# Top-k attention and squared-ReLU feed-forward: pair maxima from PSUM and SBUF, quad maxima by a reduction

## The chip, the core and the metric

The kernel runs on one core of a Trainium2 chip. The metric is the device time of one execution in microseconds; the time stated for the kernel is the median of three runs. The profile is that of one execution, taken by the hardware profiler.

## The reference

`q`, `k` and `v` have the shape 8 x 8 x 576 x 64 (batches, heads, positions, head size), in float32.

```python
scores = (1 / sqrt(64)) * q @ k.transpose(0, 1, 3, 2)      # 576 x 576 for each head
kth    = np.partition(scores, -32, axis=-1)[..., -32:-31]   # 32nd largest of each row
scores = np.where(scores >= kth, scores, -1e9)
attn   = softmax(scores)                                    # over the 32 that are left
x      = (attn @ v), heads side by side                     # 4608 x 512
out    = relu(x @ w_in) ** 2 @ w_out                        # 512 -> 2048 -> 512
```

## The kernel before

The kernel is not written as a program for each engine. It makes a list of operations (`pl.op`: engine, planned duration, priority, the tiles that it reads, writes and takes), and `Plan.schedule` runs through a plan of time in which each engine takes the ready operation with the lowest priority number whose tiles are free. The order that comes out is fixed: each engine's queue is then emitted in that order, with the semaphore waits that the tiles call for. So a planned duration changes no instruction, but it can change the order of every queue, and at run time each engine works through its queue strictly in turn.

**Blocks and groups.** A block is 128 rows of one head's score matrix (the last 64 rows of two heads share a block), so it is a tile of 128 x 576. Two heads make a pair, with nine blocks: three groups of two blocks and one group of three. There are 32 pairs, thus 128 groups and 288 blocks.

**The scores.** For each group TensorE computes the scores into PSUM, two banks for each block (288 columns in each; tiles `ss`), with priority `tg - 30`, and ScalarE copies each block to SBUF (tile `s`, L458). PSUM has eight banks, and all other matmuls (transposes, masked scores, `attn @ v`, both feed-forward products) use the same eight. There are eight `s` buffers; one is held until the mask `w` is made from it (L561).

**The 32nd largest (`top_k`, L426).** The 576 scores of a row are halves A and B.
- VectorE takes `m = max(A, B)` (L522, 288 columns), and GpSimd adds the bit patterns of A and B as integers (`t1`), so that `t1 - m` is later the smaller one of each pair.
- VectorE takes `pp`, the maximum of the two halves of `m` (L528, 144 columns), and GpSimd adds the two halves of `m` as integers (`t2`).
- The tile `f` holds 144 quad maxima, 144 losers of the second comparison (`t2 - pp`) and 288 losers of the first (`t1 - m`), the last two written by GpSimd.
- VectorE finds the eight largest of 144 (L539) and replaces them (L541), again over 144, then over 288, then the last eight over all 576 (L547, L550, L553). The last gives `kth`. One comparison at the end of the program tells whether the shortcut held for all rows; a slower second plan stands behind a branch.

The GpSimd operations are all emitted by the helper at L514. There are four buffers of `m`, `pp` and `f`, and two of `t1` and `t2`.

**The rest.** ScalarE makes `w = relu(kth - s)` (L561). `attend` computes the scores once more, transposed, adds the steep penalty of `w` by a matmul, and exponentiates (L620, L633); `attn @ v` follows, its normalisation on VectorE and GpSimd (L661, L663), and a transpose. `feed` runs the feed-forward for a batch (L698 to L741). VectorE's operations in `top_k` have rising priorities from `tg`, so a group's are planned after those of the group before.

Of the kernel before, what the change touches and what calls it, by code (L numbers as in the profile page):

```python
# [5 lines left out]
ALU = mybir.AluOpType  # L6
ACTF = mybir.ActivationFunctionType
AX = mybir.AxisListType
# [12 lines left out]
class Pool:  # L21
# [16 lines left out]
    def find(self, width):  # L38
        if width == 1:
            if not self.free:  # L40
                return None
            if self.name == "psum":
                half = [s for s in self.free if (s ^ 1) not in self.free]
                s = half[0] if half else self.free[0]
            else:
                s = self.free[0]
            self.free.remove(s)
            return s
        for s in self.free:
            if s % width == 0 and all(s + i in self.free for i in range(width)):  # L50
                for i in range(width):
                    self.free.remove(s + i)
                return s
        return None
# [21 lines left out]

class Op:
    __slots__ = ("eng", "dur", "prio", "fn", "deps", "tiles", "takes", "n", "users", "start", "end",
                 "idx", "sem", "val", "ndma", "seq", "vc", "waits", "wars", "later", "nbf")


ENGS = ("pe", "act", "dve", "gp", "sp")
# [2 lines left out]
class Plan:  # L85
    def __init__(self):
        self.ops = []

    def op(self, eng, dur, prio, fn, r=(), w=(), u=(), hold=(), take=(), after=(), order=(), sem=None, ndma=0, nbf=0.0):


        o = Op()
        o.eng, o.dur, o.prio, o.fn = eng, dur, prio, fn
        o.sem, o.ndma, o.seq, o.nbf = sem, ndma, len(self.ops), nbf
        o.takes = list(take)
        o.users = []
        o.start = o.end = o.idx = o.val = o.vc = None
        deps = set(after)
        for t in r:
            deps.update(t.writers)  # L100
        for t in u:
            deps.update(t.ops)
        for t in list(r) + list(w) + list(u) + list(hold):
            t.ops.append(o)
            t.left += 1
        for t in list(w) + list(u):
            t.writers.append(o)
        for t in o.takes:
            t.taker = o
        o.later = ({t.taker for t in list(r) + list(w) + list(u) + list(hold)} | set(order)) - deps - {o, None}  # L110
        o.deps = deps
        o.wars = list(w) + list(u)
        o.tiles = list(r) + list(w) + list(u) + list(hold)
        self.ops.append(o)
        return o

    def schedule(self, t0=0.0, latency=0.12, own=0.07):
# [7 lines left out]
        busy = {e: t0 for e in ENGS}  # L125
        order = {e: [] for e in ENGS}
# [11 lines left out]
        push(t0, "go", None)  # L138
        readyat = {o: t0 + o.nbf for o in self.ops}
        done = 0  # L140
        while events:
            t = events[0][0]
            while events and events[0][0] <= t + 1e-9:
                _, _, kind, x = heapq.heappop(events)
                if kind == "end":
                    done += 1
                    for tl in x.tiles:
                        tl.left -= 1
                        if tl.left == 0 and tl.slot is not None:
                            for i in range(tl.width):  # L150
                                tl.pool.last[tl.slot + i] = tl
                            tl.pool.give(tl.slot, tl.width)
                    for v in x.users:
                        left[v] -= 1
                        lat = own if v.eng == x.eng else latency
                        readyat[v] = max(readyat[v], t + lat)
                        if left[v] == 0:
                            push(readyat[v], "ready", v)
                elif kind == "ready":
                    heapq.heappush(ready[x.eng], (x.prio, x.seq, x))  # L160
            for e in ENGS:
                if busy[e] > t + 1e-9:
                    continue
                skipped = []
                while ready[e]:
                    item = heapq.heappop(ready[e])
                    o = item[2]
                    got = []
                    ok = True
                    for tl in o.takes:  # L170
                        s = tl.pool.take(tl)
                        if s is None:
                            ok = False
                            break
                        got.append((tl, s))
                    if not ok:
                        for tl, s in got:
                            tl.pool.undo(s, tl.width)
                        skipped.append(item)
                        continue  # L180
                    for tl, s in got:
                        tl.slot = s
                        tl.prev = []
                        for i in range(tl.width):
                            p = tl.pool.last[s + i]
                            if p is not None:
                                tl.prev.append(p)
                    o.start = t
                    hold = o.dur if e != "sp" else 0.6 * o.ndma
                    o.end = t + o.dur + (hold if e == "sp" else 0)  # L190
                    busy[e] = t + hold
                    order[e].append(o)
                    push(busy[e], "go", None)
                    push(o.end, "end", o)
                    break
                for item in skipped:
                    heapq.heappush(ready[e], item)
# [79 lines left out]
def bass_top_k_attn__then__act_relu_squared_kernel(  # L277
# [8 lines left out]
    NB, H, S, D = q.shape  # L286
    assert H == 8 and S == 576 and D == 64, (NB, H, S, D)
    HALF, QUART = S // 2, S // 4
# [49 lines left out]
    def at(t):  # L338
        return mem[t.pool.name][t.slot]

    def bank(t, i=0):
        return ps32[:, t.slot + i, :]
# [11 lines left out]
                {3: ([2, 3], True), 0: ([0], False), 1: ([1], False)}, [(256, 320), (0, 128), (128, 128)])  # L354

    PER = 3.2
    T0 = 12.0

    def mm(o, l, r, start, stop=True):
# [5 lines left out]
    def build(full, weights, pl):  # L365
# [60 lines left out]
        def top_k(gi, qk, tg, dw):  # L426
# [27 lines left out]
            pl.op("pe", 1.2, tg - 30, scores, r=[qk], w=ss[:2], take=ss[:2] + st[:2])  # L454
            if nb == 3:
                pl.op("pe", 1.2, tg - 29, scores_last, r=[qk], w=[ss[2]], take=[ss[2], st[2]])
            for i in range(nb):
                pl.op("act", .64, tg - 28 + i, lambda i=i: act.copy(  # L458
                    at(st[i])[:, :].rearrange("p (a c) -> p a c", a=2),
                    ps32[:, ss[i].slot:ss[i].slot + 2, 0:HALF]), r=[ss[i]], w=[st[i]])  # L460

            a = tile("a")
            dk = [0]
# [1 line left out]
            state["g"] += 1  # L465
            state["z"] += nb == 3

            def dve(dur, fn, **kw):
                dk[0] += 1
                return pl.op("dve", dur, tg + .34 * dk[0], fn, **kw)  # L470

            def eighth(t, i):

# [35 lines left out]
            else:  # L509
# [3 lines left out]
                def whole(dur, prio, i, op, o, x, y, **kw):  # L513
                    return pl.op("gp", dur, prio + .8 * i, lambda: gp.tensor_tensor(  # L514
                        o().bitcast(I32), x().bitcast(I32), y().bitcast(I32), op), **kw)

                low, mid = [], []
                for i in range(nb):
                    A, B = (lambda i=i: at(st[i])[:, 0:HALF]), (lambda i=i: at(st[i])[:, HALF:S])
                    M, L = (lambda i=i: at(m[i])[:, :]), (lambda i=i: at(t1[i])[:, :])  # L520
                    whole(.81, tg - 1, i, ALU.add, L, A, B, r=[st[i]], w=[t1[i]], take=[t1[i]])
                    dve(.42, lambda i=i, A=A, B=B: vec.tensor_tensor(at(m[i])[:, :], A(), B(), ALU.max),  # L522
                        r=[st[i]], w=[m[i]], take=[m[i]])
                for i in range(nb):
                    M1, M2 = (lambda i=i: at(m[i])[:, 0:QUART]), (lambda i=i: at(m[i])[:, QUART:HALF])
                    Q, L = (lambda i=i: at(pp[i])[:, :]), (lambda i=i: at(t2[i])[:, :])
                    whole(.46, tg - .5, i, ALU.add, L, M1, M2, r=[m[i]], w=[t2[i]], take=[t2[i]])
                    dve(.27, lambda i=i, M1=M1, M2=M2: vec.tensor_tensor(at(pp[i])[:, :], M1(), M2(), ALU.max),  # L528
                        r=[m[i]], w=[pp[i]], take=[pp[i], f[i]] + ([a] if i == 0 else []))
                for i in range(nb):  # L530
                    mid.append(whole(.48, tg + .5, i, ALU.subtract, lambda i=i: at(f[i])[:, QUART:HALF],
                                     lambda i=i: at(t2[i])[:, :], lambda i=i: at(pp[i])[:, :],
                                     r=[t2[i], pp[i]], w=[f[i]]))
                    low.append(whole(.88, tg + 2.5, i, ALU.subtract, lambda i=i: at(f[i])[:, HALF:S],
                                     lambda i=i: at(t1[i])[:, :], lambda i=i: at(m[i])[:, :],
                                     r=[t1[i], m[i]], w=[f[i]]))
                prev = [[] for _ in range(nb)]
# [379 lines left out]
```

## Time and profile before

| what | us |
|---|---|
| median of three runs | 1082.91 (1082.89 to 1084.41) |
| the profiled execution | 1080.87 |
| its span, first to last instruction | 1079.0 |
| VectorE busy | 980.8 |
| TensorE busy | 918.1 |
| GpSimd busy | 906.7 |
| ScalarE busy | 765.9 |

Busy is the time in which at least one instruction of the engine is in the record; successive instructions of VectorE and GpSimd overlap a little in the records, so that the distance from one start to the next is shorter than the duration of one. Durations below are those of the records unless it is said that they are distances.

### The profile page before, as it was taken

To read this page: it belongs to the slowest core of one execution; us is meant where nothing else is said; L and a number is where in the kernel's file an instruction comes from. 1 tells how busy PE (TensorE), PEld (TensorE's weight loads), DVE (VectorE), ACT (ScalarE), POOL (GpSimd) and SP (SyncE) were. 2 spreads that over 40 slices of the span, in tenths; PEclk is the share of its full clock that TensorE was granted. 3 is DMA by queue.
4 is the path that set the end of the run, shared out by engine and by line. 5 is a ranking of instruction groups with operands and counts; after the bars stand their busy time and mean duration, and the time that the engine had idled before them with its cause. 6 is when DMAs were issued, how large, how long until landed. Compare 5 with 4: busy or idle time off the path is not lost.

```text
span 1079.0 us, 23727 instructions
## 1 busy us (share of the span) xinstructions
PE 918.1 (85%) x8035; PEld 548.5 (51%) x8082; DVE 980.8 (91%) x3538; ACT 765.9 (71%) x1341; POOL 906.7 (84%) x1391
## 2 busy tenths in 40 slices
PE   6766868788899998889888899898888998979897
PEld 4434435444555555545455445555455554644554
DVE  5999999599999999599999999799998899999951
ACT  5645658766698678867688777887688776656652
POOL 7998989689988898588897999789897799999871
PEclk9878789999999999999899999999999999898999
DMA  6533310220200112112110013001220100000001
GB/s 146 130 101 100 111 46 13 56 54 21 71 12 12 53 48 57 23 42 54 28 45 2 24 51 93 23 2 52 67 50 1 44 21 16 2 1 21 21 16 38
DMA packets 124419, 47.77 MB, mean 44 GB/s; under 512 B 116608, under 2 KB 116608, under 8 KB 124288
## 3 DMA queue, kind: packets, MB, share of 16 engines
q1 hardware_dynamic: 124288, 46.16, 16.6%
q8 instruction: 65, 1.06, 0.4%
q14 instruction: 66, 0.54, 0.2%
HBM read 36.70 MB, written 9.44 MB: 43 GB/s over the span
## 4 chain that ended last, share of the span: by engine, by line
DVE 59%; POOL 13%; PE 12%; issue 10%; ACT 5%; SPq 0%; DMA 0%; POOLq 0%; DVEq 0%
DVE kth L553 15%; PE ps L360 12%; DVE c L547 11%; DVE m L522 10%; DVE f L550 8%; POOL f L514 7%; DVE pp L528 7%; POOL t L514 5%; DVE f L541 4%; DVE a L539 3%; ACT w L561 2%; ACT s L458 1%; POOL x L663 1%; PE ps L363 1%; DVE rzall L661 1%
## 5 line engine op out<-in xcount | busy, mean ns | idle before, releaser
L360 PE MATMUL ps<-qk 64*128 64x288 f32 (+7 forms) x2640 | 434.4, 443 | 60.7 <-ACT w L561 19.3
L561 ACT ACTIVATE w<-s,kth 128x576 bf16<-128x576 f32 x288 | 214.5, 771 | 137.3 <-DVE kth L553 136.9
L360 PEld LDWEIGHTS ps<-qk 64*128 64x128 f32 (+1 forms) x2640 | 216.4, 185 | 178.6 <-ACT w L561 33.3
L514 POOL TENSOR_TENSOR t<-s 128x288 int32<-128x288 int32 x288 | 234.0, 823 | 33.0 <-ACT s L458 30.5
L514 POOL TENSOR_TENSOR f<-t,m 128x288 int32<-128x288 int32 x288 | 228.1, 807 | 0.0
L514 POOL TENSOR_TENSOR t<-m 128x144 int32<-128x144 int32 x288 | 180.8, 638 | 49.9 <-DVE m L522 47.8
L550 DVE MATCH_REPLACE8 f<-c,f 128x144 f32<-128x144 f32 (+1 forms) x576 | 206.4, 363 | 0.0
L553 DVE MAX8 kth<-f 128x8 f32<-128x576 f32 x288 | 202.9, 742 | 2.6 <-POOL f L514 2.6
L620 ACT ACTIVATE p<-ps 128x640 bf16<-128x640 f32 (+1 forms) x192 | 155.2, 809 | 57.3 <-PE ps L360 56.0
L522 DVE TENSOR_TENSOR m<-s 128x288 f32<-128x288 f32 x288 | 158.8, 583 | 40.8 <-ACT s L458 40.8
L458 ACT COPY s<-ps 128x576 f32<-128x576 f32 x288 | 170.8, 642 | 33.2 <-PE ps L360 32.6
L547 DVE MAX8 c<-f 128x8 f32<-128x144 f32 (+1 forms) x576 | 190.8, 367 | 2.0 <-POOL f L514 1.9
L360 PE MATMUL ps<-wo,g 128*128 128x512 bf16 (+1 forms) x593 | 151.5, 383 | 8.7 <-ACT p L620 2.1
L360 PE MATMUL ps<-xt,win 128*128 128x288 bf16 (+2 forms) x1088 | 142.9, 284 | 7.4 <-ACT g L706 2.4
L514 POOL TENSOR_TENSOR f<-t,pp 128x144 int32<-128x144 int32 x288 | 141.7, 509 | 3.2 <-DVE pp L528 3.2
L360 PEld LDWEIGHTS ps<-steep_bf,w 128*128 128x128 bf16 (+1 forms) x1600 | 83.6, 102 | 110.4 <-issue 109.4
L528 DVE TENSOR_TENSOR pp<-m 128x144 f32<-128x144 f32 x288 | 131.5, 492 | 0.4
L360 PE MATMUL ps<-steep_bf,w 128*128 128x128 bf16 (+3 forms) x1600 | 124.0, 222 | 0.0
L360 PEld LDWEIGHTS ps<-xt,win 128*128 128x128 bf16 x1088 | 97.4, 99 | 40.0 <-ACT g L704 3.3
L360 PEld LDWEIGHTS ps<-wo,g 128*128 128x128 bf16 (+1 forms) x640 | 56.1, 101 | 60.7 <-issue 8.2
L541 DVE MATCH_REPLACE8 f<-a,pp 128x144 f32<-128x144 f32 x288 | 81.4, 287 | 0.0
L663 POOL TENSOR_TENSOR x<-av,rzall 128x256 bf16<-128x256 f32 (+2 forms) x68 | 43.7, 643 | 44.6 <-DVE rzall L661 43.9
(54 smaller groups left out, 807.7 us busy)
## 6 DMA issues: line engine op xcount, KB each, us to landing
rq<-in_q_dram SPq DMA_DIRECT2D x64, 128.0 KB, 2.4
rk<-in_k_dram SPq DMA_DIRECT2D x64, 128.0 KB, 2.5
rv<-in_v_dram SPq DMA_DIRECT2D x64, 128.0 KB, 2.3
out_dram<-o SPq DMA_DIRECT2D x32, 256.0 KB, 2.1
ws<-in_moe_w_in_dram SPq DMA_DIRECT2D x8, 512.0 KB, 4.4
ws<-in_moe_w_out_dram SPq DMA_DIRECT2D x8, 512.0 KB, 3.6
rq<-in_q_dram SPq DMA_DIRECT2D x32, 32.0 KB, 2.5
rk<-in_k_dram SPq DMA_DIRECT2D x32, 32.0 KB, 2.4
```

The costliest lines, as they stand in the source:

```text
L360: return pe.matmul(o, l, r, start=start, stop=stop, skip_group_check=True)
L458: pl.op("act", .64, tg - 28 + i, lambda i=i: act.copy(at(st[i])[:, :].rearrange("p (a c) -> p a c", a=2), ps32[:, ss[i].slot:ss[i].slot + ...
L514: return pl.op("gp", dur, prio + .8 * i, lambda: gp.tensor_tensor(o().bitcast(I32), x().bitcast(I32), y().bitcast(I32), op), **kw)
L522: dve(.42, lambda i=i, A=A, B=B: vec.tensor_tensor(at(m[i])[:, :], A(), B(), ALU.max), r=[st[i]], w=[m[i]], take=[m[i]])
L528: dve(.27, lambda i=i, M1=M1, M2=M2: vec.tensor_tensor(at(pp[i])[:, :], M1(), M2(), ALU.max), r=[m[i]], w=[pp[i]], take=[pp[i], f[i]] + ([ ...
L541: prev[i] = [dve(.275, lambda i=i: vec.match_replace(at(f[i])[:, 0:QUART], at(a)[:, i, :], at(pp[i])[:, :], NEG), r=[pp[i]], hold=[a], w=[ ...
L547: lambda i=i, t=t, wd=wd: vec.max(eighth(t, i), at(f[i])[:, 0:wd]),
L550: prev[i] = [chain(t, i, prev[i], dur + .06, lambda i=i, t=t, wd=wd: vec.match_replace(at(f[i])[:, 0:wd], eighth(t, i), at(f[i])[:, 0:wd], ...
L553: ks.append(chain(kth, i, prev[i] + [low[i]], .665, lambda i=i: vec.max(eighth(kth, i), at(f[i])[:, :]), hold=[f[i]]))
L561: pl.op("act", .75, tw + .8 * i, lambda i=i: act.activation(at(ws[i])[:, :], at(st[i])[:, :], ACTF.Relu, bias=kth[:, i, ix[i]:ix[i] + 1], ...
L620: return act.activation(o, i, ACTF.Exp, scale=0.125)
L663: pl.op("gp", .15 + .16 * nu, tt + 4, lambda: gp.tensor_tensor(at(xr)[:, 0:nu, :], at(avs)[:, 0:nu, 0:64], rzall[:, u0:u0 + nu].unsqueeze( ...
```

## The change

Pair maxima: `m` reads its first half from the score banks in PSUM and the second half from the SBUF copy. The operation now also holds the score banks (they were free after ScalarE's copy), and it still comes after that copy (`after=[cp[i]]`). Its priority is lowered by `ME = 10`, so that it is planned earlier in VectorE's queue.

Quad maxima: `pp` is a `tensor_reduce` over the innermost axis of a view of `m` with 144 pairs (the elements of a pair lie 144 columns apart), in place of a `tensor_tensor` of its two halves.

Planning: durations of several operations are restated (GpSimd's four of each block, ScalarE's all .05 less), and a wide PSUM tile takes the lowest free slot in place of the one that has been free for longest. Fields for a lock between engines (`lk`) and a width of three are added to the planner; no operation in this kernel passes them.

```diff
-        for s in self.free:
-            if s % width == 0 and all(s + i in self.free for i in range(width)):
+        for s in sorted(self.free):
+            if (width == 3 or s % width == 0) and all(s + i in self.free for i in range(width)):
...
-        o.eng, o.dur, o.prio, o.fn = eng, dur, prio, fn
+        o.eng, o.dur, o.prio, o.fn = eng, dur - (.05 if eng == "act" else 0), prio, fn
...
+    ME = 10
...
+            cp = []
             for i in range(nb):
-                pl.op("act", .64, tg - 28 + i, lambda i=i: act.copy(
+                cp.append(pl.op("act", .64, tg - 28 + i, lambda i=i: act.copy(
...
-            def dve(dur, fn, **kw):
+            def dve(dur, fn, dp=0, **kw):
                 dk[0] += 1
-                return pl.op("dve", dur, tg + .34 * dk[0], fn, **kw)
+                return pl.op("dve", dur, tg + .34 * dk[0] + dp, fn, **kw)
...
-                    whole(.81, tg - 1, i, ALU.add, L, A, B, r=[st[i]], w=[t1[i]], take=[t1[i]])
-                    dve(.42, lambda i=i, A=A, B=B: vec.tensor_tensor(at(m[i])[:, :], A(), B(), ALU.max),
-                        r=[st[i]], w=[m[i]], take=[m[i]])
+                    whole(.78, tg - 1, i, ALU.add, L, A, B, r=[st[i]], w=[t1[i]], take=[t1[i]])
+                    dve(.43, lambda i=i: vec.tensor_tensor(
+                        at(m[i])[:, :], bank(ss[i])[:, 0:HALF], at(st[i])[:, HALF:S], ALU.max), dp=-ME,
+                        r=[ss[i]], hold=[st[i]], after=[cp[i]], w=[m[i]], take=[m[i]])
...
-                    whole(.46, tg - .5, i, ALU.add, L, M1, M2, r=[m[i]], w=[t2[i]], take=[t2[i]])
-                    dve(.27, lambda i=i, M1=M1, M2=M2: vec.tensor_tensor(at(pp[i])[:, :], M1(), M2(), ALU.max),
+                    whole(.44, tg - .5, i, ALU.add, L, M1, M2, r=[m[i]], w=[t2[i]], take=[t2[i]])
+                    dve(.375, lambda i=i: vec.tensor_reduce(
+                        at(pp[i])[:, :], at(m[i])[:, :].rearrange("p (a c) -> p c a", a=2), AX.X, ALU.max),
                         r=[m[i]], w=[pp[i]], take=[pp[i], f[i]] + ([a] if i == 0 else []))
...
-                    mid.append(whole(.48, tg + .5, i, ALU.subtract, lambda i=i: at(f[i])[:, QUART:HALF],
+                    mid.append(whole(.44, tg + .5, i, ALU.subtract, lambda i=i: at(f[i])[:, QUART:HALF],
...
-                    low.append(whole(.88, tg + 2.5, i, ALU.subtract, lambda i=i: at(f[i])[:, HALF:S],
+                    low.append(whole(.78, tg + 2.5, i, ALU.subtract, lambda i=i: at(f[i])[:, HALF:S],
```

## Rows read from the trace of the kernel before

**Rows 1.** The page: span, busy time of each engine, shares of the last chain.
```profile
span 1079.0 us, 23727 instructions
...
PE 918.1 (85%) x8035; PEld 548.5 (51%) x8082; DVE 980.8 (91%) x3538; ACT 765.9 (71%) x1341; POOL 906.7 (84%) x1391
...
DVE 59%; POOL 13%; PE 12%; issue 10%; ACT 5%; SPq 0%; DMA 0%; POOLq 0%; DVEq 0%
```

**Rows 2.** Windows: length, busy of PE, PEld, DVE, ACT, POOL, clock, DMA.
```profile
200.00:220.00 20.00, 17.57 (x163) 10.91 (x163) 5.39 (x14) 16.98 (x31) 10.28 (x19) 0.97 0.40 89
...
218.00:1020.00 802.00, 709.65 (x6265) 419.87 (x6306) 768.04 (x2799) 599.39 (x1046) 693.46 (x1053) 0.98 0.13 33
```

**Rows 3.** Groups of VectorE by line and shape: busy us, mean ns, idle before.
```profile
L522 DVE TENSOR_TENSOR m<-s 128x288 f32<-128x288 f32 x288 | 158.8, 583 | 40.8 <-ACT s L458 40.8
L528 DVE TENSOR_TENSOR pp<-m 128x144 f32<-128x144 f32 x288 | 131.5, 492 | 0.4
...
L834 DVE TENSOR_REDUCE flag<-ps 1x1 int32<-1x3 f32 x1 | 0.1, 150 | 0.0
```

**Rows 4.** Single lines: shortest, median and longest duration in ns.
```profile
L522 DVE TENSOR_TENSOR m<-s x288: 420/450/1397, 11.1 to 1027.6; 128x288 f32<-128x288 f32 x144
...
L528 DVE TENSOR_TENSOR pp<-m x288: 261/589/1136, 11.6 to 1029.0; 128x144 f32<-128x144 f32 x144
...
L553 DVE MAX8 kth<-f x288: 716/743/762, 17.9 to 1046.8; 128x8 f32<-128x576 f32 x144
...
L514 POOL TENSOR_TENSOR t<-m x288: 478/552/1662, 12.1 to 1040.5; 128x144 int32<-128x144 int32 x144
```

**Rows 5.** Timeline of VectorE, 601 to 625 us: start, length, instruction.
```profile
601.01 0.80 DVE L522 TENSOR_TENSOR m<-s 128x288 f32<-128x288 f32 x2
601.73 0.51 DVE L528 TENSOR_TENSOR pp<-m 128x144 f32<-128x144 f32 x2
602.17 0.51 DVE L539 MAX8 a<-pp 128x8 f32<-128x144 f32 x2
...
604.85 0.07 DVE L550 MATCH_VALUE_LOAD f<-c,f 128x8 f32 x1
...
605.27 0.08 DVE L550 MATCH_VALUE_LOAD f<-c,f 128x8 f32 x1
...
613.04 1.17 DVE L522 TENSOR_TENSOR m<-s 128x288 f32<-128x288 f32 x3
...
622.54 1.75 DVE L522 TENSOR_TENSOR m<-s 128x288 f32<-128x288 f32 x2
624.22 1.11 DVE L528 TENSOR_TENSOR pp<-m 128x144 f32<-128x144 f32 x2
```

**Rows 6.** Timeline of GpSimd over the same stretch.
```profile
600.02 0.86 POOL L422 TENSOR_SCALAR vb<-rv,heads 128x64 bf16<-128x64 f32 x2
601.53 1.52 POOL L514 TENSOR_TENSOR t<-m 128x144 int32<-128x144 int32 x2 [0.65 <-DVE m L522]
...
622.97 1.01 POOL L514 TENSOR_TENSOR t<-s 128x288 int32<-128x288 int32 x1
```

**Rows 7.** Timeline of VectorE near the end: two reductions of 288 columns.
```profile
1054.16 0.45 DVE L826 TENSOR_REDUCE fone<-rzall 128x1 f32<-128x288 f32 x1
1054.53 0.44 DVE L827 TENSOR_REDUCE fone<-rzall 128x1 f32<-128x288 f32 x1
```

**Rows 8.** Waits of VectorE: us in total, times, longest.
```profile
DVE m L522 <- ACT s L458: 40.8, 10, 13.4
DVE rzall L661 <- ACT av L659: 28.9, 12, 7.9
```

**Rows 9.** Waits of TensorE: us in total, times, longest.
```profile
PE ps L363 <- POOL x L663: 55.7, 37, 7.3
...
PE ps L360 <- ACT p L620: 14.9, 15, 2.4
```

**Rows 10.** Timeline of ScalarE: the score copies that L522 reads at 613.04 us.
```profile
602.12 1.73 ACT L458 COPY s<-ps 128x576 f32<-128x576 f32 x3
```

More of the change, by code (lines that the diff above doesn't have):

```diff
@@ L78 @@
     __slots__ = ("eng", "dur", "prio", "fn", "deps", "tiles", "takes", "n", "users", "start", "end",
-                 "idx", "sem", "val", "ndma", "seq", "vc", "waits", "wars", "later", "nbf")
+                 "idx", "sem", "val", "ndma", "seq", "vc", "waits", "wars", "later", "nbf", "lk")
 ENGS = ("pe", "act", "dve", "gp", "sp")
@@ L87, in __init__, with op @@
         self.ops = []
-    def op(self, eng, dur, prio, fn, r=(), w=(), u=(), hold=(), take=(), after=(), order=(), sem=None, ndma=0, nbf=0.0):
+    def op(self, eng, dur, prio, fn, r=(), w=(), u=(), hold=(), take=(), after=(), order=(), sem=None, ndma=0, nbf=0.0, lk=False):
         o = Op()
-        o.eng, o.dur, o.prio, o.fn = eng, dur, prio, fn
-        o.sem, o.ndma, o.seq, o.nbf = sem, ndma, len(self.ops), nbf
+        o.eng, o.dur, o.prio, o.fn = eng, dur - (.05 if eng == "act" else 0), prio, fn
+        o.sem, o.ndma, o.seq, o.nbf, o.lk = sem, ndma, len(self.ops), nbf, lk
         o.takes = list(take)
@@ L140, in schedule @@
         done = 0
+        locked = t0
         while events:
@@ L161, in schedule @@
             for e in ENGS:
-                if busy[e] > t + 1e-9:
+                if busy[e] > t + 1e-9 or (e == "gp" and locked > t + 1e-9):
                     continue
@@ L187, in schedule @@
                                 tl.prev.append(p)
-                    o.start = t
+                    o.start = max(t, busy["gp"]) if o.lk else t
                     hold = o.dur if e != "sp" else 0.6 * o.ndma
-                    o.end = t + o.dur + (hold if e == "sp" else 0)
-                    busy[e] = t + hold
+                    o.end = o.start + o.dur + (hold if e == "sp" else 0)
+                    busy[e] = o.start + hold
+                    if o.lk:
+                        locked = o.end
                     order[e].append(o)
@@ L456, in top_k @@
                 pl.op("pe", 1.2, tg - 29, scores_last, r=[qk], w=[ss[2]], take=[ss[2], st[2]])
+            cp = []
             for i in range(nb):
-                pl.op("act", .64, tg - 28 + i, lambda i=i: act.copy(
+                cp.append(pl.op("act", .64, tg - 28 + i, lambda i=i: act.copy(
                     at(st[i])[:, :].rearrange("p (a c) -> p a c", a=2),
-                    ps32[:, ss[i].slot:ss[i].slot + 2, 0:HALF]), r=[ss[i]], w=[st[i]])
+                    ps32[:, ss[i].slot:ss[i].slot + 2, 0:HALF]), r=[ss[i]], w=[st[i]]))
             a = tile("a")
```

## The prediction

> **What bounds the kernel now.** I read the page first. VectorE is busy for 980.8 of 1079.0 us and has 59% of the chain that ended last [rows 1]. TensorE and GpSimd are at 85% and 84%, so neither is far behind. [...] Time leaves the kernel only if VectorE's 288 blocks get shorter, or if the 98 us in which it stands (1079.0 - 980.8) do.
>
> The second view is VectorE's groups by line. The two operations that the change touches take 583 and 492 ns on average [rows 3]. The single lines show that these means hide two populations: L522 ranges from 420 over a median of 450 to 1397 ns, L528 from 261 over 589 to 1136, while the MAX8 of L553 stays between 716 and 762 [rows 4]. Something lengthens exactly the operations with two SBUF sources.
>
> The timelines of VectorE and GpSimd, side by side, show what. At 601.01 us the two `m` of a group start .36 us apart, and GpSimd stands idle until 601.53, waiting for `m` [rows 5, 6]. At 622.54 us two `m` take 1.68 us to the start of `pp`, .84 each, while GpSimd works on `t1`, which there takes 1.01 us [rows 5, 6]. The GpSimd operation `t2` in turn ranges from 478 to 1662 ns [rows 4]. So each holds the other up.
>
> The waits are the last view. VectorE waits 40.8 us in ten waits for score copies and 28.9 us in twelve for `attn @ v` [rows 8]. One stretch is 200 to 220 us, in which it works only 5.39 us [rows 2].
>
> **The change part by part.** The reference point for undisturbed operations is the group at 601.01 us. `m`: distance .36 us, so a duration of .80 - .36 = .44 us. `pp`: the two `pp` start at 601.73 and the next MAX8 at 602.17, so a distance of .22 and a duration of .51 - .22 = .29 us [rows 5].
>
> *Removed: the hold-ups.* For `m` the mean is 583 ns, 143 above 440; times 288 that is 41.2 us. For `pp` it is 492, 202 above 290; times 288 that is 58.2 us [rows 3, 5]. Together 99.4 us of VectorE. This asks that neither new form is held up. The reduction has one source, like the MAX8 whose duration doesn't move [rows 4]; `m` with one source in PSUM has no row here, and I come back to it among the rivals. [...]
>
> *Added: the reduction.* L826 and L827 reduce 288 columns each, contiguous and to one value; their starts are .37 us apart [rows 7]. The new `pp` reads as many columns but writes 144 values. At .37 against .22 us it costs .15 x 288 = 43.2 us. From below it can't be under .22, the cost of the 144 results alone (0 us). From above, if the small groups don't stream and the 144 results cost as much again, it is .37 + .22 = .59, or 106.6 us. I take .37: it is the row with the same operation and the same number of elements read.
>
> *Added: the PSUM source of `m`.* The only VectorE row from PSUM is L834, 150 ns for three elements in one partition [rows 3]. A surcharge is hard to see in it: at 1.10 ns a column, from (420 - 261)/144 of the shortest rows [rows 4], the 450 ns of a reduction of 288 columns [rows 7] leave 133 ns fixed, and these 150 leave 147. That bounds it from below at nothing. From above I take the slowest 288-column step that is never held up, value load and replacement: 604.85 to 605.27 us, .42 [rows 5], thus .06 x 288 = 17.3 us. I take the upper end, since one stream from each memory is unlikely to start faster than two from one.
>
> [...]
>
> *Sum on VectorE:* 99.4 - 43.2 - 17.3 = 38.9 us less. The bounds are 56.2 without a surcharge, and -24.5 (a loss) with the dear reduction.
>
> *GpSimd* keeps all its instructions and loses its share of the hold-ups (`t2` has a median of 552 over a shortest of 478 [rows 4]). It is not the bound, so I count nothing. If it were late, VectorE's last MAX8 of a block would wait for `f`; with 693.5 us in 802 [rows 2] it has room.
>
> *Moved: `m` ten us of priority earlier, and the score banks held until it.* ScalarE's copy stays, since `w` and the second half of `m` need it, so ScalarE and the DMA queues lose nothing. New is that TensorE's next use of a score bank waits for `m` on VectorE. Queued behind that are all of TensorE's matmuls: attention, feed-forward, the next scores. And `m` sits earlier in VectorE's queue: now its copies end at 603.85 us and it starts at 613.04, 9.2 us of slack [rows 5, 10]. Planned earlier, a late copy would stop VectorE in the middle of a group that could have gone on. Both cost nothing as long as TensorE is ahead. With 38.9 x 768/981 = 31 us out of the middle stretch (its share of VectorE's busy time [rows 1, 2]), TensorE's share rises from 709.7/802 = 88% to 709.7/771 = 92%, so it is ahead by less. If the waits for score copies other than the start (40.8 less the 11.1 us before the first `m` [rows 4, 8], 29.7 us) grow with the reciprocal of TensorE's free share, (1 - .885)/(1 - .920) = 1.44, they grow by 13 us. From below they don't grow at all, because the queues are planned anew. This is an estimate from those rows; I take the middle, 6.5 us.
>
> *The rest* (restated planned durations, lowest free PSUM slot) changes only orders. It is in that same unknown: I can't read the new order from a trace of the old one.
>
> **Total.** The profiled execution took 1080.87 us, 1.9 around its span; 1080.9 - 38.9 + 6.5 = 1048.5. The median of the runs is 2.0 higher, so I say 1050.5.
>
> **The rivals.**
>
> *Better: no surcharge, fewer stalls.* Without the 17.3 us the time is 1033; if the new order also keeps the long stalls out it falls towards 1015. For it: the low end of the surcharge from L834, and that some stalls, as the 14.6 us from 200 to 220, look like accidents of the order [rows 2]. Against: the surcharge has only that one row, and a busier TensorE.
>
> *Eaten by stalls:* VectorE gains 39 us but waits eat 22 to 37 of it: 1066 to 1081. For it: VectorE's ten waits for copies show that the supply of scores is at times short already [rows 8].
>
> *Slower: the score banks.* Scores are given out long before their turn, and now four (or six) of eight banks stay taken until `m` gets a free `m` buffer, which comes only when GpSimd is done with an earlier group. The other matmuls share what is left. For it: TensorE already waits 14.9 us in 15 waits for ScalarE to clear `p`, 1.0 us each [rows 9]. One more wait of that length in every second of 128 groups, passed on to VectorE, is 64 us: 1082.9 - 38.9 + 64 = 1108. It decides from 38.9/128 = .30 us for each group. Against: TensorE's largest wait, 55.7 us, is for work that follows VectorE [rows 9], and would shrink. [...]
>
> *Slower: the dear reduction.* At .59 us the sum is +24.5 instead of -38.9 us: 1082.9 + 24.5 + 6.5 = 1114. For it: no row has short groups with a stride. Against: the undisturbed steps of 288 columns all lie at .36 to .42 us [rows 5, 7].
>
> *The change doesn't do what it says:* `m` is still held up although a source is in PSUM. Then 41.2 us come back: 1050.5 + 41.2 = 1092, or 1074 without the surcharge. Against: the constant MAX8, which reads SBUF as well, by one source.
>
> **How the numbers follow.** Chances: forecast (1036 to 1066) .50, better (below 1036) .17, eaten by stalls .09, score banks .15, dear reduction .05, `m` still held up .04. The predicted time is the forecast's, 1050.5. The range is 1030 to 1090: below it lies about a third of the better case (.06), above it the dear reduction, half of the score banks and a little of the last, together about .19 outside. A difference of .2% (2.2 us) is about what a measurement of this kernel can tell from none. Faster: .50 + .17, most of the .09 and half of the last, .76. Same: the edges of the stalls and of the banks, .04. Slower: .20.
>
> **What would show it.** In the new profile `m` should lie at about .44 to .52 us and `pp` at about .45 us, both with a narrow spread, whatever GpSimd does; `t2` should fall towards 480 ns. VectorE's busy time should fall to about 942 us. The dear reduction shows as a `pp` over .55 us. [...] The banks show as waits of TensorE for L522's successor and as waits of `m` for copies above 41 us, with more idle windows on VectorE. I would be wrong first in the stalls: the order of every queue is new.

## The result and the profile after

The changed kernel takes 1006.14 us (median of four runs, 1005.36 to 1009.17) against 1082.97 of the kernel before: a ratio of .9293, 95% interval .9272 to .9314. That is 76.8 us less, where 32 were forecast, and below the range of 1030 to 1090. The profiled execution took 1005.76 us.

The page of the changed kernel, with the same lines as [rows 1]:

```profile
span 1003.8 us, 23634 instructions
...
PE 910.8 (91%) x8082; PEld 537.9 (54%) x8082; DVE 927.3 (92%) x3538; ACT 765.0 (76%) x1341; POOL 836.6 (83%) x1391
...
POOL 36%; DVE 26%; PE 19%; issue 12%; ACT 5%; SPq 1%; DMA 1%; POOLq 0%; DVEq 0%
```

VectorE is busy for 53.5 us less (980.8 to 927.3), and it stands for 76.5 us (1003.8 - 927.3) where it stood for 98.2. These two, 53.5 and 21.7, are the 75.2 us by which the span is shorter. GpSimd is 70.1 us less busy with the same 1391 instructions. The last chain now runs through GpSimd more than through VectorE (36% against 26%), though VectorE is the busier one; the chain alone does not show which of the two bounds the kernel.

The groups of VectorE and GpSimd in the changed kernel, as in [rows 3] (line, operation, busy us, mean ns, idle before):

```profile
L528 DVE TENSOR_TENSOR m<-ps,s 128x288 f32<-128x288 f32 x288 | 126.8, 447 | 22.0 <-ACT s L464 18.2 <-POOL f L520 2.1
...
L535 DVE TENSOR_REDUCE pp<-m 128x144 f32<-128x288 f32 x288 | 116.1, 445 | 0.1
...
L520 POOL TENSOR_TENSOR t<-m 128x144 int32<-128x144 int32 x288 | 141.4, 492 | 2.3
L520 POOL TENSOR_TENSOR f<-t,pp 128x144 int32<-128x144 int32 x288 | 135.7, 489 | 99.4 <-DVE pp L535 99.2
```

And their shortest, median and longest durations, as in [rows 4]:

```profile
L528 DVE TENSOR_TENSOR m<-ps,s x288: 418/447/462, 11.2 to 946.3; 128x288 f32<-128x288 f32 x144
...
L535 DVE TENSOR_REDUCE pp<-m x288: 418/446/461, 11.7 to 949.9; 128x144 f32<-128x288 f32 x144
...
L520 POOL TENSOR_TENSOR t<-m x288: 477/491/512, 12.0 to 948.5; 128x144 int32<-128x144 int32 x144
```

The tails are gone on both engines: `m` ends at 462 ns where it went to 1397, `t2` at 512 where it went to 1662. Counted one by one in the traces, 158 of the 288 `m` before start while an instruction of GpSimd is under way and take 698 ns on average; the other 130 take 443, the longest 459. Now 271 start so, and they take 446 ns on average.

The waits of the changed kernel, VectorE's as in [rows 8] and TensorE's as in [rows 9]:

```profile
DVE rzall L669 <- ACT av L667: 27.0, 11, 6.3
DVE m L528 <- ACT s L464: 18.2, 10, 11.2
...
PE ps L365 <- DVE m L528: 36.2, 45, 3.5
PE ps L368 <- POOL x L671: 9.4, 7, 2.9
PE ps L365 <- ACT p L628: 9.0, 16, 1.3
PE ps L368 <- DVE m L528: 8.9, 7, 2.7
```

VectorE waits 18.2 us for score copies instead of 40.8, and this fall of 22.6 us is about as much as the whole standing lost. TensorE has the new wait that was feared, 36.2 + 8.9 = 45.1 us for `m` to clear the score banks. At the same time its wait for the normalised `x`, which follows VectorE and GpSimd, fell from 55.7 [rows 9] to 9.4 us.

### The profile page after: what moved, and what is told of

It is laid out like the page before. It is cut to its first block, busy times and chain, and to the rows that moved or that the text cites. A ratio compares the mean times of both kernels' runs of the same rounds, so it can differ in the third digit from the quotient of the medians.

```text
span 1003.8 us, 23634 instructions
## 1 busy us (share of the span) xinstructions
PE 910.8 (91%) x8082; PEld 537.9 (54%) x8082; DVE 927.3 (92%) x3538; ACT 765.0 (76%) x1341; POOL 836.6 (83%) x1391
## 4 chain that ended last, share of the span: by engine, by line
POOL 36%; DVE 26%; PE 19%; issue 12%; ACT 5%; SPq 1%; DMA 1%; POOLq 0%; DVEq 0%
POOL f L520 18%; PE ps L365 18%; POOL t L520 13%; DVE kth L561 6%; DVE f L558 5%; DVE c L555 4%; DVE m L528 4%; DVE pp L535 3%; POOL x L671 2%; DVE f L549 2%; DVE a L547 2%; POOL vb L427 1%; ACT w L569 1%; ACT s L464 1%; ACT p L628 1%
## 5 line engine op out<-in xcount | busy, mean ns | idle before, releaser
L365 PEld LDWEIGHTS ps<-qk 64*128 64x128 f32 (+1 forms) x2640 | 212.9, 181 | 169.8 <-DVE m L528 57.7
L520 POOL TENSOR_TENSOR t<-s 128x288 int32<-128x288 int32 x288 | 229.2, 797 | 9.9 <-ACT s L464 7.5
L520 POOL TENSOR_TENSOR f<-t,m 128x288 int32<-128x288 int32 x288 | 223.9, 795 | 0.0
L520 POOL TENSOR_TENSOR f<-t,pp 128x144 int32<-128x144 int32 x288 | 135.7, 489 | 99.4 <-DVE pp L535 99.2
L365 PE MATMUL ps<-wo,g 128*128 128x512 bf16 (+1 forms) x640 | 158.8, 381 | 0.6 <-ACT xt L688 0.5
L528 DVE TENSOR_TENSOR m<-ps,s 128x288 f32<-128x288 f32 x288 | 126.8, 447 | 22.0 <-ACT s L464 18.2
L520 POOL TENSOR_TENSOR t<-m 128x144 int32<-128x144 int32 x288 | 141.4, 492 | 2.3
L535 DVE TENSOR_REDUCE pp<-m 128x144 f32<-128x288 f32 x288 | 116.1, 445 | 0.1
L712 ACT ACTIVATE g<-ps 128x576 bf16<-128x576 f32 x112 | 71.9, 654 | 7.9 <-PE ps L365 6.8
```

The lines of the kernel that those rows point to most:

```text
L365: return pe.matmul(o, l, r, start=start, stop=stop, skip_group_check=True)
L528: dve(.43, lambda i=i: vec.tensor_tensor(at(m[i])[:, :], bank(ss[i])[:, 0:HALF], at(st[i])[:, HALF:S], ALU.max), dp=-ME, r=[ss[i]], hold=[ ...
L535: dve(.375, lambda i=i: vec.tensor_reduce(at(pp[i])[:, :], at(m[i])[:, :].rearrange("p (a c) -> p c a", a=2), AX.X, ALU.max), r=[m[i]], w= ...
L712: return act.activation(at(g)[:, 0:nt].rearrange("p (a c) -> p a c", a=2), ps32[:, hh.slot:hh.slot + 2, 0:hw], ACTF.Relu)
```

## The experiments

The theory, my reading of [rows 4] (VectorE's operations with a tail have two SBUF sources, the MAX8 with one has none), is that VectorE and GpSimd hold each other up when both read SBUF by more than one stream, and that the time follows from taking this away. The rival is that the new order of the queues gives most of it. Every kernel below is the changed kernel with the edit shown, except the one that is called the kernel before with one line changed. The diffs are shortened, and of GpSimd's operations, `m` and `pp` some give only the planned durations. "Standing" is the span less VectorE's busy time in the profiled execution. Each ratio is to executions of the kernel before taken beside that run, whose medians lie between 1082.97 and 1086.2 us.

| edit to the changed kernel | us | ratio to before (95%) | VectorE busy | standing |
|---|---|---|---|---|
| (kernel before) | 1082.97 | 1 | 980.8 | 98.2 |
| (changed kernel) | 1006.14 | .9293 (.9272 to .9314) | 927.3 | 76.5 |
| both old operands | 1069.76 | .9860 (.9843 to .9876) | 986.9 | 81.0 |
| old planning | 1056.21 | .9744 (.9727 to .9760) | 930.8 | 123.2 |
| ME = 0 | 1020.16 | .9408 (.9392 to .9423) | 926.7 | 89.8 |
| oldest slot | 1003.39 | .9248 (.9232 to .9263) | 927.1 | 74.5 |
| old quad maxima | 997.06 | .9195 (.9174 to .9216) | 911.0 | 81.0 |
| old pair maxima | 1075.73 | .9924 (.9901 to .9948) | 1001.3 | 71.3 |
| old plan of ScalarE and GpSimd | 1032.54 | .9515 (.9491 to .9539) | 924.2 | 106.3 |
| old plan of `m` and `pp` | 1017.72 | .9383 (.9364 to .9403) | 922.9 | 91.8 |

**Operands against order.** The first run keeps every queue's order and puts the old operands back; the second keeps the new operands and puts the planning back.

```diff
-   at(m[i])[:, :], bank(ss[i])[:, 0:HALF], at(st[i])[:, HALF:S], ALU.max)
+   at(m[i])[:, :], at(st[i])[:, 0:HALF], at(st[i])[:, HALF:S], ALU.max)
-   vec.tensor_reduce(at(pp[i])[:, :], at(m[i])[:, :].rearrange("p (a c) -> p c a", a=2), AX.X, ALU.max)
+   vec.tensor_tensor(at(pp[i])[:, :], at(m[i])[:, 0:QUART], at(m[i])[:, QUART:HALF], ALU.max)
```

> The changed kernel with its planning kept in full (every engine's queue in the new order, the score banks still held until the pair maxima), but with the old operands: pair maxima from two SBUF sources, quad maxima by tensor_tensor. Hold-up theory (the gain is the time for which VectorE and GpSimd kept each other waiting): VectorE's busy time goes back by about 53 us to 980, the long tails of both operations and of GpSimd's t2 return, and the time is 1055 to 1080. Order theory (most of the gain is the new order of the queues): the time stays below 1035.

```diff
-    ME = 10
+    ME = 0
-  o.dur = dur - (.05 if eng == "act" else 0)        # in effect
+  o.dur = dur
-  GpSimd .78 .44 .44 .78, m .43, pp .375            # planned durations
+  GpSimd .81 .46 .48 .88, m .42, pp .27
-        for s in sorted(self.free):
+        for s in self.free:
```

> The new operands, but the planning of before: old planned durations, pair maxima not moved ahead, old choice of PSUM slots; only the holding of the score banks is new there. Hold-up theory: VectorE is busy for 927 us, the standing stays near the 98 us of before, and the time is about 1030. Order theory: above 1045. If the early pair maxima are what makes the held banks harmless, the time is above 1045 too, with TensorE's waits for the pair maxima far above 45 us.

With the old operands in the new order the time is 1069.76 us: the hold-up theory's number. VectorE's two groups in that run:

```profile
L528 DVE TENSOR_TENSOR m<-s 128x288 f32<-128x288 f32 x288 | 203.8, 715 | 33.2 <-ACT s L464 16.8 <-POOL f L520 16.1
...
L535 DVE TENSOR_TENSOR pp<-m 128x144 f32<-128x144 f32 x288 | 93.9, 365 | 0.1
```

The hold-ups are back, but they have moved: in the new order `m` takes 715 ns on average (583 before) and `pp` only 365 (492 before). The trace shows why: in the new order 259 of the 288 `m` start while GpSimd has an instruction under way (158 before) and only 120 of the `pp` (262 before). Those `m` take 745 ns on average and those `pp` 468; the others take 450 and 291. So where the two engines hold each other up depends here on what stands beside what.

With the new operands in the old planning, VectorE's busy time falls by 50.0 us (980.8 to 930.8) and the time by only 28, to 1056.21 (the kernel before took 1084.5 beside it): the standing rises from 98.2 to 123.2 us, and half the gain is given back there. Its waits, VectorE's and TensorE's:

```profile
DVE m L528 <- ACT s L464: 52.0, 12, 11.3
DVE rzall L669 <- ACT av L667: 35.3, 16, 6.3
...
PE ps L365 <- DVE m L528: 67.5, 61, 6.1
PE ps L368 <- DVE m L528: 17.9, 8, 6.7
```

This time is the order theory's (above 1045), and the sign of the third expectation is there too: TensorE waits 85.4 us for `m`. As the run before gave the hold-up theory's number, neither theory accounts for both runs; both causes are at work. The operands alone give 28 us (old planning), the planning alone 15 us (old operands), and both together 77. Both together are worth more than the sum of the two.

**Which edit is it?** Each operand put back alone, in the same order (the diffs are the two halves of the first one).

> The changed kernel and its order, but the pair maxima from two SBUF sources again; the quad maxima by the reduction. If the hold-ups of the pair maxima are what the change removes: a mean of 700 ns as in the run with both old operands, VectorE 75 us busier at about 1003, and 1075 to 1095, slower than with both old operands. If the two edits are about equal in worth: 1035 to 1050.

> The changed kernel and its order, but the quad maxima by tensor_tensor from two SBUF sources again. In the run with both old operands this operation took 365 ns on average, less than the 445 of the reduction, since in the new order GpSimd mostly waits for it. If that holds: VectorE is busy for about 23 us less, 904, and the time is 980 to 995. If the quad maxima are a source of hold-ups that the reduction removes: above 1006, with a mean of the quad maxima above 445 ns.

In this order the pair maxima are everything: put back, the time is 1075.73, and `m` takes 698 ns on average. The quad maxima work the other way: put back, the time falls to 997.06, a little above the 980 to 995 that were expected. The `pp` of that run:

```profile
L535 DVE TENSOR_TENSOR pp<-m x288: 264/300/1187, 11.8 to 938.3; 128x144 f32<-128x144 f32 x144
```

Its median is 300 ns and its mean 376, against 445 for the reduction that is never held up. GpSimd waits for `pp` 89 times in that run (78.0 us), and it is idle at the start of 161 of the 288 `pp`, which take 295 ns on average; the other 127 take 480. The reduction buys certainty at a price above what the hold-ups cost here. Both predicted sizes were near: 75 us busier for `m` was 74.0, and 23 less busy for `pp` was 16.3.

**Is it GpSimd's reading?** The kernel with both old operands, with GpSimd's four operations of each block writing the same tiles without reading anything. This kernel leaves the losers of the comparisons out of the search; its time is of one execution.

```diff
-   lambda: gp.tensor_tensor(o().bitcast(I32), x().bitcast(I32), y().bitcast(I32), op)
+   lambda: gp.memset(o(), NEG)
```

> The run with both old operands and the new order, but the four GpSimd operations of each block only write (a memset of the same tiles to a very small number, with the same waits); the losers of the comparisons are left out of the search. If VectorE's operations with two SBUF sources are held up by GpSimd's reads: pair maxima near 440 ns and quad maxima near 295 on average, with short tails from the few GpSimd operations that still read, where they took 715 and 365. If any GpSimd work holds them up: tails above 500 ns stay in a large part, means of 500 and more for the pair maxima.

```profile
L527 DVE TENSOR_TENSOR m<-s 128x288 f32<-128x288 f32 x288 | 134.2, 471 | 21.8 <-ACT s L464 19.4 <-POOL f L520 0.8
...
L534 DVE TENSOR_TENSOR pp<-m 128x144 f32<-128x144 f32 x288 | 76.6, 307 | 0.1
...
L520 POOL MEMSET f<- 128x288 f32 x288 | 90.6, 338 | 0.0
```

The two-source operations, unchanged, fall from 715 and 365 to 471 and 307 ns. GpSimd is also less busy in this run (422.5 us for 908.2), so fewer of its operations could meet them; but a memset still runs 1152 times, and of the excess of `m` over 440 ns only 31 of 275 are left. The fewer meetings are not the reason, as the `m` taken one by one show: 106 overlap memsets and no other work of GpSimd, and they take 431 to 459 ns, as do the 124 that overlap nothing (429 to 460). The other 58 overlap an operation of GpSimd that still reads (casts of `v` and of the weights, the normalisation, products of the feed-forward); they take 575 ns on average and 1294 at most. An `m` that overlaps nothing but a cast of the weights, which has one source, still takes up to 1145 ns, so GpSimd need not read two streams for the hold-up, as the theory had it.

**Early pair maxima and the PSUM slot.**

```diff
-    ME = 10
+    ME = 0
```

> The changed kernel with ME = 0: the pair maxima have the priority of before, the banks are held longer. If the early pair maxima matter: 1020 to 1045, TensorE's waits for them well above 45 us and VectorE standing longer. If not: within 0.5% of 1006.

```diff
-        for s in sorted(self.free):
+        for s in self.free:
```

> The changed kernel with the old choice of PSUM slots (the pair that has been free longest, not the lowest). Both theories: within 0.5% of 1006. If the slots matter: above 1015.

Without the early pair maxima the kernel is 14 us slower. TensorE's waits for `m` are 15.6 us longer in sum (51.9 + 8.8 = 60.7 us against 45.1) and sit in 36 waits rather than 52, up to 6.5 us each; VectorE stands 13.3 us longer. The slots are worth some 3 us, and the other way: the oldest is the better one.

**What in the planning?** Each kind of planned duration put back alone.

```diff
-  o.dur = dur - (.05 if eng == "act" else 0)        # in effect
+  o.dur = dur
-  GpSimd .78 .44 .44 .78
+  GpSimd .81 .46 .48 .88
```

> The changed kernel with the old planned durations of ScalarE and GpSimd. If a plan whose durations agree with the chip makes the better order: slower, 1010 to 1030. If these durations don't matter: within 0.5% of 1006.

```diff
-  m .43, pp .375
+  m .42, pp .27
```

> The changed kernel with the old planned durations of pair and quad maxima (.42 and .27, together .115 us short of the chip for each block). If it is these that made the stalls of the run with the old plan: 1020 to 1040, with VectorE standing 15 to 35 us longer. If not: within 0.5% of 1006.

> The changed kernel with only ScalarE's planned durations as before (GpSimd's are the new ones): splits the 26 us of the run with both old. If GpSimd's overstated durations made the loss: within 1% of 1006. If ScalarE's did: 1025 to 1035. About half would say that any distance from the chip's durations costs.

In the third only ScalarE's line of the diff is put back. All three are slower: 1032.54 (a little above what was expected), 1017.72 (12 us, a little under it), and with only ScalarE's restored 1044.79 (ratio .9640, .9624 to .9656), 12 us slower still than with GpSimd's restored too. The last falls above both theories' numbers and shows that these effects don't add. No instruction differs in any of them, only the order.

Whether the order is better for a reason, or by luck, was then asked by steps of one quantity (two executions for each step).

```diff
-  o.dur = dur - (.05 if eng == "act" else 0)        # in effect
+  o.dur = dur - (.02 if eng == "act" else 0)        # and .04, .06, .08
```

> The changed kernel with ScalarE's planned durations .02 us below those of before (the change takes .05, the run with 1045 us took 0). If nearness to the chip makes the order good (score copies start .54 us apart, w .67; planned .62 and .73 here): between 1045 and 1006, about 1030. If the order is luck: anywhere between 1000 and 1045, in no order among these four runs.

> The same with .04 less. Nearness to the chip: 1006 to 1015. Luck: anywhere between 1000 and 1045.

> The same with .06 less. Nearness to the chip: 1000 to 1006. Luck: anywhere between 1000 and 1045.

> The same with .08 less, which is nearest to the chip's distances (.56 planned for a copy against .54). Nearness to the chip: 1000 or below. Luck: anywhere between 1000 and 1045.

| ScalarE's plan less | 0 | .02 | .04 | .05 | .06 | .08 |
|---|---|---|---|---|---|---|
| us | 1044.8 | 1028.4 | 1015.6 | 1006.1 | 1003.8 | 1004.2 |
| standing | 113.2 | 97.8 | 87.2 | 76.5 | 73.9 | 73.8 |

It is a smooth slope with a flat floor, not a scatter. The floor is a miss of the nearness theory: it asked for 1000 or below at .08, the plan nearest to the chip. The timeline of ScalarE in the changed kernel shows on which side the chip lies:

```profile
600.46 2.11 ACT L569 ACTIVATE w<-s,kth 128x576 bf16<-128x576 f32 x3 [1.26 <-DVE kth L561]
...
602.94 1.18 ACT L464 COPY s<-ps 128x576 f32<-128x576 f32 x2
```

Two copies in 1.18 us, .64 each, start .54 us apart; three `w` in 2.11 us, .776 each, .67 apart. The planned .64 and .75 were about the durations of the records, which overlap; with .06 to .08 less the plan nears the distances, and there the floor begins. No step went past the distances, so these runs do not tell a plan near to the chip from a plan that is merely shorter for ScalarE. The waits of VectorE tell where a plan with a slow ScalarE costs time on the chip; first the run with 0, then the one with .08:

```profile
DVE m L528 <- ACT s L464: 40.8, 11, 11.2
...
DVE c L555 <- POOL f L520: 11.4, 6, 5.7
```

```profile
DVE m L528 <- ACT s L464: 16.6, 8, 11.4
...
DVE c L555 <- POOL f L520: 6.1, 5, 2.0
```

Of the 39.4 us by which the standing of the two differs, 24.2 are waits for score copies and 5.3 are waits for `f`. How the longer durations bring the copies late was not followed through the plan.

**The old operands with ScalarE's plan alone.** The kernel before with one line changed.

```diff
-        o.eng, o.dur, o.prio, o.fn = eng, dur, prio, fn
+        o.eng, o.dur, o.prio, o.fn = eng, dur - (.05 if eng == "act" else 0), prio, fn
```

> The kernel before with only ScalarE's planned durations .05 less. If ScalarE's overstated durations cost the same whatever the operands: 1045 to 1065. If it takes VectorE and GpSimd free of hold-ups, so that the plan as a whole holds on the chip: within 1% of 1084.

1064.21 us (ratio .9822, .9806 to .9838), with a standing of 81.5 us instead of 98.2: within the first expectation's range. ScalarE's .05 us is worth 20 us with the old operands; with the new ones it is worth 39 (1044.79 against 1006.14), so it does not cost the same whatever the operands, as that expectation's condition had it.

**Towards a faster version.** Pair maxima as changed, quad maxima by tensor_tensor and the oldest slot, in three plans.

```diff
-   dve(.375, ... vec.tensor_reduce(...))
+   dve(.29, ... vec.tensor_tensor(...))      # first; .375 in the second and third
-        for s in sorted(self.free):
+        for s in self.free:
```

> The pair maxima from PSUM and SBUF, the quad maxima by tensor_tensor as before with a planned duration of .29 (the distance it should have in the new order is .30, 376 ns less an overlap of 77), and the old choice of PSUM slots: what the runs so far point to as the fastest. If the gains of the two add up: 997 - 3 = 994, and some less if the better planned duration keeps stalls out (985 to 994). If the order is only luck from plan to plan: anywhere between 990 and 1020.

> Pair maxima from PSUM and SBUF, quad maxima by tensor_tensor, the planned duration of the quad maxima left at .375, and the old choice of PSUM slots. It stands between the run of 997 (lowest slot) and the run of 1003 (oldest slot, planned duration .29). If the better planned duration spoiled the order: 994 or below, with VectorE standing near 81 us. If the slots did: about 1003, with VectorE standing near 93 us.

> The run of 994 us (pair maxima from PSUM and SBUF, quad maxima by tensor_tensor, oldest slot) with ScalarE's planned durations .06 less. If the valley carries over: 990 to 994. If not: above 998.

| plan | us | ratio (95%) | VectorE busy | standing |
|---|---|---|---|---|
| `pp` .29 | 1003.35 | .9255 (.9233 to .9277) | 907.0 | 93.2 |
| `pp` .375 | 994.45 | .9177 (.9157 to .9198) | 909.0 | 84.1 |
| `pp` .375, ScalarE .06 less | 1002.88 | .9256 (.9240 to .9271) | 907.8 | 90.1 |

The second is the fastest version that keeps the whole computation, 11.7 us below the changed kernel. The first and the third are misses. A planned .29 is nearer than .375 to the distance at which `pp` mostly runs (a median of 300 ns less the overlap), and yet it is slower by 9 us; and ScalarE's floor doesn't carry over. So nearness to the chip fits the large steps of ScalarE's plan alone, and within some 10 us the order is not explained by these runs.

## Why the prediction was wrong

**The bound and the mechanism were right.** In `top_k`, no operation of VectorE but the two with two SBUF sources had a tail before (the MAX8 of L553 lies between 716 and 762 ns [rows 4]), and the tails are gone. The new `m` lies in the forecast window (.44 to .52; 447 ns), and so does `pp` (.45; 445). That neither new form is held up was an assumption: of `m` with its other source in PSUM there was no row, and the MAX8 was the only row set beside the reduction. The trace now shows it: `m` takes 462 ns at most and `pp` 461, though 271 of the `m` and 119 of the `pp` start while an instruction of GpSimd is under way. With memsets in place of GpSimd's four operations, which read, `m` with two SBUF sources falls from 715 to 471 ns.

**The surcharge was mis-sized.** I took the upper bound, 17.3 us, for the source in PSUM. Measured: 447 against 440 ns, 7 x 288 = 2.0 us (the 130 undisturbed `m` of before average 443). The step was too dear by 15.3 us. The row that pointed to next to nothing, L834 at 150 ns, had been read and put aside. With 2.0 instead of 17.3 the sum is 54.2 us; VectorE's busy time fell by 53.5.

**The stalls failed in sign.** The step was "if the waits for score copies [...] grow with the reciprocal of TensorE's free share [...] they grow by 13 us [...] I take the middle, 6.5 us". The standing fell by 21.7 us. That is 28.2 us, the larger part of the miss. The size of the step itself held: with new operands in the old planning the waits for score copies grow by 11.2 us (40.8 to 52.0), inside the 0 to 13. The standing grows by 25.0 there, since waits for `attn @ v`, for `f` and for the feed-forward grow as well; whether a shorter lead of TensorE or the held banks make these waits is not separated. What failed is that the new planning was put at nothing: the restated durations "change only orders" and went into the same unknown, and the earlier `m` was counted only as a risk. The planning as a whole takes the standing from 123.2 to 76.5 us, 46.7 us less. Put back alone, ScalarE's durations bring it to 113.2, those of `m` and `pp` to 91.8, and the old place of `m` to 89.8. Before, the planner thought ScalarE slower than it is and VectorE faster: `m` and `pp` were planned with .69 us together and took 583 + 492 ns on average. The diff showed every one of these numbers, and the trace the durations to set against them; what that would be worth, no row showed. The case "better: no surcharge, fewer stalls" is the one that came, and further than its 1015.

**The hold-ups were booked to the wrong edit.** I gave `pp` 58.2 us of hold-ups for 43.2 of price, a gain of 15. The 58.2 belong to the order of before, in which `pp` follows `m` at once and 262 of 288 meet an instruction of GpSimd; in the new order the reduction costs 9 us against the plain operation (1006.14 against 997.06, and 1003.39 against 994.45 with the oldest slot). The whole came out right all the same: both operations are free of hold-ups in the changed kernel, so VectorE loses those of before, wherever the new order would have put them. With the old operands the new order has them at `m` (275 ns each) and few at `pp` (75 ns each, 21.6 us), so the reduction had less to save than its price.

**The rivals.** The score banks: the waits came as described, 45.1 us on TensorE, and were not passed on to VectorE; TensorE's waits for work that follows VectorE shrank by as much (55.7 to 9.4). How little they are passed on, the run with the old pair maxima shows: TensorE waits 97.0 us for `m` there, and VectorE's standing is the lowest of all, 71.3 us.

```profile
PE ps L365 <- DVE m L528: 83.2, 95, 4.5
...
PE ps L368 <- DVE m L528: 13.8, 10, 2.9
```

What shows of this rival is that moving `m` ahead matters: without it the time is 14 us longer, 1020.16 us. The dear reduction did not come: 445 ns against the 453 of a contiguous one (L826 of before). That `m` would still be held up did not come either.

## What to carry to other kernels

When means of a group hide a wide spread next to a narrow one of its neighbours, compare the two engines' timelines: here moving one source to PSUM took the hold-ups away (1397 ns at most before, 462 after) at 7 ns an operation. In a kernel whose queues are ordered from planned durations, those durations are part of the program: compare them with the distance from start to start, which is shorter here than the recorded duration (.54 us against .64 for a score copy), try some values, and after an edit that makes operations steady, plan anew. The value nearest to the trace was not always the best: for `pp` .375 beat .29 by 9 us. And check an edit that comes in a bundle alone: one half of this one cost 9 us.

## What the runs showed that was not expected

A VectorE operation with one source in PSUM and one in SBUF took 447 ns for 288 columns, against 440 for two undisturbed SBUF sources (443 on average over the 130 `m` of before that start beside no instruction of GpSimd). A reduction over 144 pairs 144 columns apart took no longer than a contiguous one of 288 columns (445 against 453 ns). GpSimd's memsets, 1152 of them, left the two-source operations of VectorE undisturbed (106 `m` beside memsets alone: 431 to 459 ns). And .05 us in one engine's planned durations, with not one instruction different, moved a kernel of 1 ms by 20 us with the old operands and by 39 with the new.
